# Reads of the turned softmax blocks: four reads to 96 partitions and one to 32, in place of four to 32

## The chip, the cores and the metric

The kernel runs on one core of a Trainium2 chip. The metric is the time of one execution on the device in microseconds (us). TensorE (PE) does the matrix products; VectorE (DVE), ScalarE (ACT) and GpSimd (POOL) do the elementwise work; SyncE (SP) issues every transfer, and 16 DMA engines of the core carry them out.

## The reference: what is computed

Attention with rotary positions for 8 batches x 8 heads, 576 positions, head size 64, and on its output a channel mix, all in float32:

```python
q_rot, k_rot = rotate(q), rotate(k)
scores = scale * q_rot @ k_rot.T;  attn = softmax(scores);  x = attn @ v      # per batch and head
x_prev = x shifted by one position                                            # 512 channels
xk = mu_k * x + (1 - mu_k) * x_prev;   xr = mu_r * x + (1 - mu_r) * x_prev
k = relu(xk @ w_k);  v = (k * k) @ w_v;  r = sigmoid(xr @ w_r);  out = r * v
```

## The kernel before, in words

Heads are worked in pairs, 32 pairs in all (8 batches x 4). For a pair, `plan_prep` loads and rotates keys and queries; `plan_unit` makes the scores on PE (L417) in nine tiles of 128 queries x 576 keys (five blocks of query columns, `c` = 0 to 4, two heads each, the last shared by both), takes the row maximum on DVE (L428) and the exponential on ACT (L438).

PE needs these exponentials with the keys on partitions, so they have to be turned. For the first four pairs (`EARLY`) PE turns them itself. For the other 28 pairs DVE turns them only within blocks of 32x32 (L443), into a tile `p` of 128 partitions x 18 blocks x `WG[g]` numbers, and the rest of the turning is done by a round trip through memory in `plan_move`:

- `move_out` (L504) writes `p` to a DRAM tile `turned`, 128 rows of 18 blocks. This is done in two parts a pair, `g` = 0 (block columns 0 and 1, 128 numbers a block, 1152 KB) and `g` = 1 (2, 3 and 4; 160 numbers a block, 1440 KB).
- `move_in` (L509) reads it back into a tile `rows`, where a partition holds one key position of a block. There are four reads a part, one for each strip of 32 partitions. Blocks are dealt to the strips as 5, 5, 4 and 4 (`STRIPS`).

`rows` then is the moving operand of the product with the values (PE `av`, L534; 20 matmuls a part), and its result is divided by the row sums (`rb`, loaded by DMA from a small DRAM tile `inv`). There is one `rows` tile per part and one `p` tile per part, so the reads of a part for the next pair wait until PE has consumed this pair's, and two DRAM tiles `turned` per part. The channel mix (L614 to L616, three products for each of its matrices, high and low halves) of a batch runs between the attention of the next one.

What sets the order: nothing is scheduled by the hardware. `Plan.issue` plays the program through with the costs and latencies in `Plan.LATENCY`, `act`, `dve`, `pool` and in `Plan.dma` (rate and issue cost of a transfer), and takes the ready operation with the lowest rank; ranks are made from the tables `R`, `EARLY_R`, `PB`, `MB` and the `B_` numbers. The order it finds is the order in which the instructions are written out for each engine, and each engine runs its own list strictly in that order. All transfers are in the list of SP. Besides the waits for their data, the transfers of the built program share eight semaphores in turn, so a transfer is issued only when the one eight places ahead of it has landed.

On the host, `value_blocks` lays out the values' rows in the order in which `rows` holds the key positions.

Of the kernel before, what the change touches and what calls it, by code (L numbers as in the profile page):

```python
# [22 lines left out]
P = 128  # L23
# [1 line left out]
PLAIN = 9  # L25
GROUPS = ((0, 1), (2, 3, 4))
WG = (128, 160)
STRIPS = ((0, 5), (5, 5), (10, 4), (14, 4))
EARLY = 4
R = dict(k=-170.58, q=-121.86, v=-302.6, cs=1164.53, mu=991.11, ld=1958.72, rope0=549.92, rope1=1861.93,  # L30
         rope2=137.07, split0=1585.28, split1=-369.49, u0=-285.6, u1=-146.91, u2=-135.16, u3=-245.03, u4=-224.69,
         mx=-295.32, ex=-799.79, tp=638.63, di=170.09, dm=471.79, da=86.98, dw=-1486.25, dr2=1804.88, av=1680.01,
         ah=108.11, nr=-491.67, ev=-709.36, m0=142.77, mh=-13.55, mk=-153.7, mr=282.14, ms=158.17, mx1=-19.12,
         mx2=219.25, mx3=-908.53, mg=21.82, mv=16.35, dr=-380.32, key0=-1186.84, key1=1101.65, key2=400.27,
         gate0=1557.76, gate1=-659.69, wk0=-28.46, wk1=-245.65, wr0=-326.36, wr1=175.07, wv0=-137.55, wv1=337.66)
EARLY_R = dict(k=-564.0, q=-1170.11, v=-343.8, ld=-1562.58, rope0=293.9, rope1=424.08, rope2=-27.38,
               split0=-678.82, split1=947.24, u0=48.92, u1=-764.8, u2=-518.62, u3=-170.28, u4=-518.36, mx=320.33,
               ex=-960.19, tp=-251.82, di=-478.7, dm=-397.13, da=-510.21, dw=-405.45, dr2=471.62, av=-248.39,
               ah=506.21, nr=448.89, ev=-1023.97)
PB = (-1701.39, 236.47, -547.89, 58.95, 176.83, -159.49, -34.46, 8.57)  # L40
B_COPY, B_ROPE, B_SPLIT, B_LOW, B_MIX, B_SQUARE, B_RELU = -1101.5, -35.23, 368.36, 1453.79, 1150.37, -1080.99, -375.92
MB = (-168.94, -271.8, -134.14, -339.86, 331.16, -643.19, 619.37, 428.48)
CY = 12
BUFS = dict(nat=2, kh=2, kl=1, qh=2, ql=1, vs=1, pe=4, pe3=8, p0=1, p1=1, s=2, s3=3, nm=6, sums=2, rb=1, pt0=1, pt1=1, t=2, xT=5, raw=1, we=1, wm=1, mxf=2, mxh=5, mxl=5, acc=2, hr=2, kkh=8, kkl=8, rt=3)

# [5 lines left out]
def act(n):  # L51
    return 0.833 * n + 100


def dve(n):
    return 1.04 * n + 70


def dve2(n):
    return 0.52 * n + 75  # L60
# [12 lines left out]
class Plan:  # L73
# [16 lines left out]
    def op(self, engine, rank, cost, fn, after=(), uses=()):  # L90


        o = len(self.ops)
        if isinstance(engine, str):
            engine, fn = {engine: (cost, 0, engine == "G")}, lambda e, fn=fn: fn()
        opens = [s for s in uses if s.opener is None]
        for s in uses:
            s.users += 1
        for s in opens:
            s.opener = o  # L100
        self.ops.append((engine, rank, None, fn, tuple(after), tuple(uses), opens))
        return o

    def dma(self, rank, nbytes, fn, after=(), uses=(), rate=360):

        o = self.op("S", rank, 610, fn, after, uses)
        return self.op("D", rank, nbytes / rate, lambda: None, [o], uses)

    def issue(self):
# [92 lines left out]
def rope_attention_channel_mix(ctx, tc, qt, kt, v, cs, mu, w_k, w_v, w_r, out):  # L202
# [3 lines left out]
    nc = tc.nc  # L206
    B, NP, _, _, S = kt.shape
# [32 lines left out]
    def one(n, bias=0.0):  # L240

        return {"A": (act(n) + 30, 0, False), "V": (dve2(n), bias, True)}
# [8 lines left out]
    op, dma, Slot = plan.op, plan.dma, plan.slot  # L251
# [24 lines left out]
    rows_t = [const.tile([P, 4, 5, n], F32, name=f"rows_{n}") for n in WG]  # L276
# [98 lines left out]
    def plan_prep(t, b, g):  # L375
        d = live[b, g]
        d["r"] = EARLY_R if PAIRS.index((b, g)) < EARLY else R
        d["bg"], d["plain"] = (b, g), PAIRS.index((b, g)) < PLAIN
        first = PAIRS[0] == (b, g)
        plan_rope(t + d["r"]["k"], d, "k", kt[b, g], tables["cs"], d["plain"], -339.0 if first else t + d["r"]["k"] + d["r"]["ld"])  # L380
        plan_rope(t + d["r"]["q"], d, "q", qt[b, g], tables["cs"], d["plain"], -289.0 if first else t + d["r"]["q"] + d["r"]["ld"])
        sv = d["sv"] = Slot("vs")

        def load_v():
            d["vf"] = values_t[sv.index % BUFS["vs"]]
            nc.sync.dma_start(d["vf"], v[b, g])

        d["v"] = dma(t + d["r"]["v"] + d["r"]["ld"], P * 4 * 10 * D, load_v, [], [sv])
# [83 lines left out]
    def plan_move(t, d):  # L472


        ss, sr = d["ss"], Slot("rb")
        w = {}

        def inverse():
            V.tensor_scalar_add(d["sums"][:, 0:9], d["sums"][:, 0:9], 1e-9)
            V.reciprocal(d["sums"][:, 0:9], d["sums"][:, 0:9])  # L480
            V.tensor_copy(d["sums"][:, 9:10], d["sums"][:, 4:5])
            V.transpose(d["sums"], d["sums"])

        def write():
            w["dram"] = dram.tile([4, 32, 32], F32, tag="inv", name="inv", bufs=4)
            nc.sync.dma_start(w["dram"].rearrange("a u n -> (a u) n"), d["sums"])

        def read(x):
            if "rb" not in d:
                d["rb"] = sb.tile([P, 4, 160], F32, tag="rb", name="rb", bufs=BUFS["rb"])  # L490
            src = w["dram"][:, 5 * x:5 * x + 5, :].rearrange("a u n -> a (u n)").unsqueeze(0).to_broadcast([D, 4, 160])
            nc.sync.dma_start(d["rb"][(up, dn)[x]], src)

        o = op("V", t + d["r"]["nr"], 500, inverse, [d["E", u] for u in range(9)], [ss])
        o = dma(t + d["r"]["dw"], P * 128, write, [o], [ss])
        d["R"] = [dma(t + d["r"]["dr2"] + 0.1 * x, D * 4 * 640, lambda x=x: read(x), [o], [sr]) for x in range(2)]
        d["sr"] = sr

        if d["early"]:
            return  # L500

        def move_out(g):
            w["p", g] = dram.tile([P, 18, WG[g]], F32, tag=f"turned{g}", name="turned", bufs=2)
            nc.sync.dma_start(w["p", g].rearrange("p b n -> p (b n)"), d["p", g].rearrange("p b n -> p (b n)"))  # L504

        def move_in(g, s):
            at, n = STRIPS[s]
            src = w["p", g].rearrange("(a i) b n -> i a (b n)", a=4)[:, :, at * WG[g]:(at + n) * WG[g]]
            nc.sync.dma_start(rows_t[g][32 * s:32 * s + 32, :, 0:n, :].rearrange("p a j n -> p a (j n)"), src)  # L509

        for g, cs in enumerate(GROUPS):
            ready = [d["T", u] for c in cs for u in ((4,) if c == 4 else (c, c + 5))]
            o = dma(t + d["r"]["dm"] + d["r"]["da"] * g, P * 18 * 4 * WG[g], lambda g=g: move_out(g), ready, [d["sp", g]])
            for s in range(4):
                d["M", g].append(dma(t + d["r"]["dm"] + d["r"]["da"] * g + d["r"]["di"], P * STRIPS[s][1] * 4 * WG[g], lambda g=g, s=s: move_in(g, s), [o], [d["spt", g]]))

    N0 = S // 2

    def plan_values(t, d):
# [4 lines left out]
        for g in range(2):  # L524
# [18 lines left out]
            def divided_last(x):  # L543
                r = (up, dn)[x]
                acc = w[1][:, 0:384].rearrange("p (a n) -> p a n", a=4)[r, :, 80 - 80 * x:96 - 80 * x]
                V.tensor_tensor(out=d["x"][r, 513:S + 1].rearrange("p (a n) -> p a n", n=16), in0=acc, in1=d["rb"][r, :, 128 + 16 * x:144 + 16 * x], op=ALU.mult)

            o = op("T", t + d["r"]["av"] + d["r"]["ah"] * g, 2350 + 540 * g, products, d["M", g] + [d["v"]], [s_a, d["sv"], d["spt", g]])
            e[g] = [op("V", t + d["r"]["ev"] + d["r"]["ah"] * g, dve(256) + 30, divided, [o] + d["R"], [s_a, sx, d["sr"]])]
            if g:  # L550
                e[g] += [op("V", t + d["r"]["ev"] + d["r"]["ah"] * g + 0.1 * x, dve(64) + 30, lambda x=x: divided_last(x), [o] + d["R"], [s_a, sx, d["sr"]]) for x in range(2)]
        z = op("G", t + d["r"]["ev"], 110, lambda: G.memset(d["x"][:, 0:1], 0.0), [], [sx])
        d["X", 0], d["X", 1] = e[0] + e[1] + [z], e[0] + e[1]

    def plan_attention():
        for pi, bg in enumerate(PAIRS):
            plan.group = 2 * pi
            d, t = live[bg], PT * pi + (PB[pi] if pi < len(PB) else 0)
            plan_prep(t, *bg)
# [4 lines left out]
            for c in range(5):  # L564
                plan.group = 2 * pi + 0.1 * c
                plan_unit(t + (EARLY_R if pi < EARLY else R)[f"u{c}"], d, c)
            plan.group = 2 * pi
# [7 lines left out]
    def plan_mix(t, b, half, which, f, hold):  # L575
# [24 lines left out]
        o = op({"A": (act(n) + 130, 0, False), "V": (dve2(n) + 60, B_MIX, True)}, t, 0, previous, d["X", half] + [rest], [sx, s_f])  # L600
        o = op({"V": (dve(n) + 60, 0, True)}, t + R["mx1"], 0, mixed, [o], [sx, s_f])
        h = op(one(n, B_SPLIT), t + R["mx2"], 0, high, [o], [s_f, s_h])
# [102 lines left out]
    for b in range(B):  # L705
        plan_channel_mix(b, 4 * PT * b + R["m0"] + MB[b], 4 * PT * (b + 1) + R["m0"] + MB[b])
    with tc.manual_schedule():
# [65 lines left out]
```

## Time and profile before

| | |
|---|---|
| median of 3 runs | 1089.62 us (1087.89 to 1099.95) |
| the profiled execution's own time | 1090.39 us |
| its span, first to last instruction | 1088.6 us |
| PE busy | 958.2 us (88%) |
| DVE / ACT / POOL busy | 75% / 51% / 46% |
| DMA traffic | 231.72 MB, 213 GB/s over the span, 75.2% of the 16 engines' time |
| mean granted TensorE clock | 0.953 of full speed |

The span is what the profile's times are counted in; the profiled execution's own time is 1.8 us more. DMA's share is the mean over the 16 engines: it says how long packets were under way, not how fast they went, so it is read beside the GB/s of the same stretch.

### The profile page before, as it was taken

How to read it: one execution, taken by the hardware profiler on the slowest of the kernel's cores; microseconds unless marked ns; L12 is line 12 of the kernel's file. 1: busy time of each engine (PE TensorE's matmuls, PEld its weight loads, DVE VectorE, ACT ScalarE, POOL GpSimd, SP SyncE). 2: the span in 40 equal slices, each digit the busy share in tenths (PEclk: the TensorE clock that was granted, in tenths of full speed). 3: DMA queues.
4: the chain of work that ended last, by engine and by line, in shares of the span. 5: the costliest groups of instructions: out<-in, count | busy, mean ns of one | idle time of the engine just before them, and what ended most of it. 6: DMA issues, size and time to landing. Idle time of an engine off the chain costs nothing.

```text
span 1088.6 us, 18700 instructions
## 1 busy us (share of the span) xinstructions
PE 958.2 (88%) x6866; PEld 778.6 (72%) x6866; DVE 816.1 (75%) x1419; ACT 551.0 (51%) x1356; POOL 498.9 (46%) x502
## 2 busy tenths in 40 slices
PE   2788778658979999989999999999999999988898
PEld 1454456437758888868888888777777978777888
DVE  6998997798866798767988899869786966434542
ACT  2566645445454566545656665547545653414133
POOL 4644356643464474545645465529353742201111
PEclk9999879757999999999999999999999999999999
DMA  5434499964899769998998799998999597790000
GB/s 183 156 126 158 131 300 292 289 225 162 216 265 257 194 221 248 236 276 259 292 307 237 241 225 273 262 288 268 266 279 272 187 240 214 179 221 11 11 23 22
DMA packets 92731, 231.72 MB, mean 213 GB/s; under 512 B 13152, under 2 KB 37728, under 8 KB 85472
## 3 DMA queue, kind: packets, MB, share of 16 engines
q1 hardware_dynamic: 92640, 230.53, 75.2%
q8 instruction: 54, 0.88, 0.4%
q14 instruction: 37, 0.30, 0.1%
HBM read 146.21 MB, written 84.28 MB: 212 GB/s over the span
## 4 chain that ended last, share of the span: by engine, by line
PE 60%; DMA 20%; DVE 13%; ACT 3%; issue 3%; POOL 1%; SPq 1%; DVEq 0%; ACTq 0%; POOLq 0%
PE scores L614 14%; PE av L534 12%; PE scores L616 11%; PE scores L615 11%; PE scores L417 9%; DMA rows<-turned 8%; DVE nm L428 2%; DVE p L443 2%; DMA rb<-inv 2%; DMA values<-in_v 2%; DMA out_dram<-rt 2%; DMA xk<-in_kt 2%; DMA turned<-p 2%; PE turn L463 1%; DMA xq<-in_qt 1%
## 5 line engine op out<-in xcount | busy, mean ns | idle before, releaser
L438 ACT ACTIVATE pe<-scores,nm 128x576 f32<-128x576 f32 x252 | 184.6, 737 | 121.3 <-DVE nm L428 117.2
L428 DVE TENSOR_REDUCE nm<-scores 128x1 f32<-128x576 f32 x288 | 205.5, 747 | 38.8 <-PE scores L417 37.8
L443 DVE STREAM_TRANSPOSE p<-pe 128x576 f32<-128x576 f32 x252 | 186.3, 760 | 10.5 <-ACT pe L438 10.1
L534 PE MATMUL av<-rows,values 128*64 128x320 f32 (+1 forms) x1280 | 175.3, 423 | 20.4 <-issue 5.2
L417 PE MATMUL scores<-kh,qh 64*128 64x288 f32 x738 | 145.3, 428 | 48.8 <-ACT pe L438 29.6
L614 PE MATMUL scores<-mxh,wk_h 128*128 128x288 f32 x496 | 156.8, 316 | 14.7 <-ACT hr L631 7.6
L614 PE MATMUL scores<-kkh,wv_h 128*128 128x288 f32 x480 | 148.0, 308 | 14.3 <-ACT rt L661 8.2
L254 POOL TENSOR_TENSOR mxl<-mxf,mxh 128x288 fp32r<-128x288 f32 x90 | 78.7, 876 | 173.0 <-ACT mxh L258 143.3
L534 PEld LDWEIGHTS av<-rows,values 128*64 128x64 f32 x1280 | 91.8, 141 | 83.9 <-issue 31.0
L417 PEld LDWEIGHTS scores<-kh,qh 64*128 64x128 f32 x738 | 81.7, 207 | 98.0 <-ACT pe L438 41.9
L615 PE MATMUL scores<-mxl,wk_h 128*128 128x288 f32 x496 | 146.9, 296 | 1.1 <-POOL mxl L254 1.1
L616 PE MATMUL scores<-mxh,wk_l 128*128 128x288 f32 x496 | 146.6, 296 | 0.0
L616 PE MATMUL scores<-kkh,wv_l 128*128 128x288 f32 x480 | 143.4, 299 | 1.5 <-POOL wv_l L254 1.5
L615 PE MATMUL scores<-kkl,wv_h 128*128 128x288 f32 x480 | 143.1, 298 | 0.0
L254 POOL TENSOR_TENSOR kkl<-hr,kkh 128x288 fp32r<-128x288 f32 x101 | 90.0, 902 | 90.2 <-ACT kkh L258 67.8
L614 PEld LDWEIGHTS scores<-mxh,wk_h 128*128 128x128 f32 x496 | 93.8, 189 | 37.1 <-ACT hr L631 13.1
L254 POOL TENSOR_TENSOR xk<-xk,turns 128x576 f32<-128x576 f32 x46 | 70.9, 1553 | 91.4 <-DMA xk<-in_kt 73.7
L614 PEld LDWEIGHTS scores<-kkh,wv_h 128*128 128x128 f32 x480 | 91.6, 191 | 27.4 <-ACT rt L661 13.7
L254 POOL TENSOR_TENSOR xq<-xq,turns 128x128 f32<-128x128 f32 (+1 forms) x96 | 98.9, 1048 | 17.5 <-DMA xq<-in_qt 17.5
L590 DVE SCALAR_TENSOR_TENSOR mxf<-xT,mu_t,mxf 128x288 f32<-128x288 f32 x128 | 90.1, 718 | 10.7 <-ACT mxf L585 10.0
L615 PEld LDWEIGHTS scores<-mxl,wk_h 128*128 128x128 f32 x496 | 94.0, 189 | 1.5 <-POOL mxl L254 1.3
L616 PEld LDWEIGHTS scores<-mxh,wk_l 128*128 128x128 f32 x496 | 93.8, 189 | 0.2 <-POOL wk_l L254 0.2
(110 smaller groups left out, 1860.9 us busy)
## 6 DMA issues: line engine op xcount, KB each, us to landing
turned<-p SPq DMA_DIRECT2D x28, 1440.0 KB, 8.1
rows<-turned SPq DMA_DIRECT2D x112, 320.0 KB, 9.8
turned<-p SPq DMA_DIRECT2D x28, 1152.0 KB, 6.8
rows<-turned SPq DMA_DIRECT2D x56, 400.0 KB, 8.8
xq<-in_qt SPq DMA_DIRECT2D x32, 640.0 KB, 6.6
xk<-in_kt SPq DMA_DIRECT2D x32, 576.0 KB, 5.2
rows<-turned SPq DMA_DIRECT2D x56, 256.0 KB, 9.0
values<-in_v SPq DMA_DIRECT2D x32, 320.0 KB, 6.3
```

What stands on the lines that cost most here:

```text
L254: (V if e == "V" else G).tensor_tensor(out=out, in0=a, in1=b, op=op)
L417: T.matmul(w[x][:, h, 0:H], lhsT=kind(d[q][r, c * P:(c + 1) * P]), rhs=kind(d[k][r, h * H:(h + 1) * H]), start=i == 0, stop=i == len(todo) ...
L428: V.tensor_reduce(out=w["nm", x], in_=w[x][:, :, 0:H], op=ALU.max, axis=AX.XY, negate=True)
L438: A.activation(w["p", x].rearrange("p (h n) -> p h n", h=2), w[x][:, :, 0:H], AF.Exp, bias=w["nm", x], scale=1.0, accum_out=d["sums"][:, u ...
L443: V.transpose(d["p", g][:, :, at:at + 32], w["p", x].rearrange("p (b n) -> p b n", n=32))
L463: T.transpose(a[i][0:n, k * P:(k + 1) * P], w["p", x][:, j * P:j * P + n], early["ident"])
L534: T.matmul(acc[(up, dn)[x], :, to:to + n], lhsT=d["vf"][:, 5 * x + j, :], rhs=rows_t[g][:, :, j, n * x:n * x + n], start=j == 0, stop=j == 4)
L590: V.scalar_tensor_tensor(out=x["f"], in0=d["x"][:, half * n + 1:half * n + n + 1], scalar=mu_t[:, m:m + 1], in1=x["f"], op0=ALU.mult, op1= ...
L614: T.matmul(w["a"], lhsT=w_h[:, i, sl], rhs=x["h"], start=(i == 0), stop=False)
L615: T.matmul(w["a"], lhsT=w_h[:, i, sl], rhs=x["l"], start=False, stop=False)
L616: T.matmul(w["a"], lhsT=w_l[:, i, sl], rhs=x["h"], start=False, stop=(i == count - 1))
```

## The change

`move_in` reads a part with five transfers in place of four. Blocks are dealt to the strips as 5, 5, 5 and 3. For each of the four groups of 32 rows of `turned` (`a` = 0 to 3) one wide read takes blocks 0 to 14 to partitions 0 to 95; a fifth, narrow read takes blocks 15 to 17 of all rows to partitions 96 to 127. The host lays out the values to suit. `Plan.dma` now counts 400 bytes a nanosecond and 500 ns an issue (360 and 610 before), and all numbers of the rank tables are new, so the written order of every engine is new. The products, the elementwise work and the bytes moved are the same; some elementwise operations change engine. `STRIPS` was the constant `((0, 5), (5, 5), (10, 4), (14, 4))`.

```diff
-    def dma(self, rank, nbytes, fn, after=(), uses=(), rate=360):
+    def dma(self, rank, nbytes, fn, after=(), uses=(), rate=400):
-        o = self.op("S", rank, 610, fn, after, uses)
+        o = self.op("S", rank, 500, fn, after, uses)
...
-R = dict(k=-170.58, q=-121.86, v=-302.6, cs=1164.53, ...
+R = dict(k=-46.24, q=-112.99, v=167.3, cs=1791.75, ...
...
-        def move_in(g, s):
-            at, n = STRIPS[s]
-            src = w["p", g].rearrange("(a i) b n -> i a (b n)", a=4)[:, :, at * WG[g]:(at + n) * WG[g]]
-            nc.sync.dma_start(rows_t[g][32 * s:32 * s + 32, :, 0:n, :].rearrange("p a j n -> p a (j n)"), src)
+        def move_in(g, a):
+            rows = w["p", g].rearrange("(a i) b n -> i a b n", a=4)
+            if a < 4:
+                src = rows[:, a, 0:15].rearrange("i (s j) n -> s i (j n)", s=3)
+                nc.sync.dma_start(rows_t[g][0:96, a].rearrange("p j n -> p (j n)"), src)
+            else:
+                nc.sync.dma_start(rows_t[g][96:128, :, 0:3].rearrange("p a j n -> p a (j n)"), rows[:, :, 15:18].rearrange("i a j n -> i a (j n)"))
...
-            for s in range(4):
+            for a in range(5):
...
-        rows = np.full((4, 5, 32), S)
-        for s, (at, n) in enumerate(STRIPS):
-            rows[s, :n] = 32 * at + np.arange(32 * n).reshape(n, 32)
+        rows = np.minimum(32 * np.arange(20).reshape(4, 5, 1) + np.arange(32), S)
```

The new order shows best in SP's list, which holds every transfer. In its rows `turned<-p` is `move_out`, `rows_85<-turned` is a read of part 0 and `rows_86<-turned` one of part 1; the figures are the destination's partitions and numbers. The first place is the first pairs that move through memory. Before, SP's list read:

```order
L492 DMA rb<-inv 64x4x160 x2
L504 DMA turned<-p 128x2880
L504 DMA turned<-p 128x2304
L291 DMA raw<-in_w_v 128x1024
L509 DMA rows_86<-turned 32x4x800 x2
L509 DMA rows_86<-turned 32x4x640 x2
L509 DMA rows_85<-turned 32x4x640 x2
L509 DMA rows_85<-turned 32x4x512 x2
```

At the same place it now reads:

```order
L491 DMA rb<-inv 64x4x160 x2
L290 DMA raw<-in_w_r 128x1024
L503 DMA turned<-p 128x2880
L503 DMA turned<-p 128x2304
L509 DMA rows_86<-turned 96x1x800 x4
L511 DMA rows_86<-turned 32x4x480
L290 DMA raw<-in_w_v 128x1024
L509 DMA rows_85<-turned 96x1x640 x4
L511 DMA rows_85<-turned 32x4x384
```

Both writes still stand ahead of the reads of either part; each part has five reads where it had four, and one load of weights moved from between writes and reads to between the two parts' reads.

The second place lies in the middle of the program. Before, with one pair's part 1 and the next pair's part 0:

```order
L504 DMA turned<-p 128x2880
L386 DMA values_84<-in_v 128x640
L509 DMA rows_86<-turned 32x4x800 x2
L509 DMA rows_86<-turned 32x4x640 x2
L492 DMA rb<-inv 64x4x160 x2
L504 DMA turned<-p 128x2304
L509 DMA rows_85<-turned 32x4x640 x2
L509 DMA rows_85<-turned 32x4x512 x2
```

Now, at about the same pair:

```order
L503 DMA turned<-p 128x2880
L509 DMA rows_85<-turned 96x1x640 x4
L511 DMA rows_85<-turned 32x4x384
L385 DMA values_84<-in_v 128x640
L491 DMA rb<-inv 64x4x160 x2
L509 DMA rows_86<-turned 96x1x800 x4
L511 DMA rows_86<-turned 32x4x480
L673 DMA out_dram<-rt 128x288
L503 DMA turned<-p 128x2304
```

The write of part 1 now stands ahead of part 0's five reads, and the write of the next pair's part 0 stands behind part 1's five reads, where it stood behind four.

More of the change, by code (lines that the diff above doesn't have):

```diff
@@ L27 @@
 WG = (128, 160)
-STRIPS = ((0, 5), (5, 5), (10, 4), (14, 4))
 EARLY = 4
[L30 to L41, printed above, removed]
@@ L42 @@
-MB = (-168.94, -271.8, -134.14, -339.86, 331.16, -643.19, 619.37, 428.48)
+R = dict(k=-46.24, q=-112.99, v=167.3, cs=1791.75, mu=1264.72, ld=1640.88, rope0=668.83, rope1=2170.31,
+         rope2=211.53, split0=2202.72, split1=-693.2, u0=-108.39, u1=-45.48, u2=97.67, u3=-159.77, u4=-101.54,
+         mx=-380.59, ex=-996.03, tp=699.01, di=289.95, dm=353.77, da=300.36, dw=-1881.33, dr2=1719.07, av=2521.55,
+         ah=37.68, nr=-329.79, ev=-753.5, m0=163.4, mh=-16.68, mk=-24.16, mr=458.27, ms=166.92, mx1=123.09,
+         mx2=293.74, mx3=-969.99, mg=19.94, mv=13.82, dr=-638.28, key0=-1508.07, key1=1346.18, key2=6.54,
+         gate0=1608.26, gate1=-632.21, wk0=-90.95, wk1=-286.28, wr0=-674.72, wr1=347.38, wv0=-150.67, wv1=699.56)
@@ new lines @@
+EARLY_R = dict(k=-310.88, q=-1355.07, v=-331.38, ld=-1622.22, rope0=79.01, rope1=567.18, rope2=2.18,
+               split0=-1418.42, split1=1048.63, u0=262.56, u1=-1137.39, u2=-761.37, u3=-324.26, u4=-789.59,
+               mx=563.5, ex=-1246.54, tp=-462.09, di=-476.12, dm=-336.66, da=-381.54, dw=-472.89, dr2=453.49,
+               av=-108.63, ah=991.69, nr=711.42, ev=-1376.42)
+PB = (-2105.41, -72.54, -662.78, -122.25, 227.08, -309.22, -249.69, -51.84)
+B_COPY, B_ROPE, B_SPLIT, B_LOW, B_MIX, B_SQUARE, B_RELU = -971.16, -56.64, 275.68, 1563.02, 1219.56, -1021.28, -501.08
@@ L43 @@
+MB = (-91.7, -221.08, 59.62, -939.17, 511.62, -723.89, 612.38, 501.23)
 CY = 12
@@ L513, in plan_move @@
             o = dma(t + d["r"]["dm"] + d["r"]["da"] * g, P * 18 * 4 * WG[g], lambda g=g: move_out(g), ready, [d["sp", g]])
-            for s in range(4):
-                d["M", g].append(dma(t + d["r"]["dm"] + d["r"]["da"] * g + d["r"]["di"], P * STRIPS[s][1] * 4 * WG[g], lambda g=g, s=s: move_in(g, s), [o], [d["spt", g]]))
+            for a in range(5):
+                d["M", g].append(dma(t + d["r"]["dm"] + d["r"]["da"] * g + d["r"]["di"], (96 * 5 if a < 4 else 32 * 24) * 4 * WG[g], lambda g=g, a=a: move_in(g, a), [o], [d["spt", g]]))
     N0 = S // 2
```

## The prediction

> **What bounds the kernel now.** First the page: busy shares, the forty slices' DMA rows, the queue, and the shares of the chain that ended last.
>
> ```profile
> span 1088.6 us, 18700 instructions
> PE 958.2 (88%) x6866; PEld 778.6 (72%) x6866; DVE 816.1 (75%) x1419; ACT 551.0 (51%) x1356; POOL 498.9 (46%) x502
> DMA  5434499964899769998998799998999597790000
> q1 hardware_dynamic: 92640, 230.53, 75.2%
> PE 60%; DMA 20%; DVE 13%; ACT 3%; issue 3%; POOL 1%; SPq 1%; DVEq 0%; ACTq 0%; POOLq 0%
> ```
>
> PE is busy for 88% and carries 60% of the chain, so TensorE sets most of the time; but DMA is second, and in the middle of the program its engines are nearly as full. So next come the transfers by group (count, KB each, us from issue to landing), and what waits for the reads that the change rewrites.
>
> ```profile
> turned<-p SPq DMA_DIRECT2D x28, 1440.0 KB, 8.1
> rows<-turned SPq DMA_DIRECT2D x112, 320.0 KB, 9.8
> turned<-p SPq DMA_DIRECT2D x28, 1152.0 KB, 6.8
> rows<-turned SPq DMA_DIRECT2D x56, 400.0 KB, 8.8
> rows<-turned SPq DMA_DIRECT2D x56, 256.0 KB, 9.0
> ...
> L509 SPq DMA_DIRECT2D rows<-turned x224: 302/430/1662, 132.4 to 968.7; - x112
> ...
>   PE av L534: 9.7, 6
> ```
>
> A read of 320 KB takes longer to land than a write of 1152 KB; yet PE waited for reads only 9.7 us in all (last row: us, times). The reads are slow but mostly hidden: there is little to win on them, and much to lose if they become the bound. How fast the DMA engines go shows in stretches where one kind of transfer rules (after the length: busy us and counts of PE, PEld, DVE, ACT and POOL, granted clock, DMA share, GB/s):
>
> ```profile
> 144.00:149.00 5.00, 2.67 (x16) 1.44 (x14) 4.97 (x9) 2.22 (x5) 3.65 (x5) 1.00 1.05 388
> 154.00:161.00 7.00, 5.95 (x33) 5.05 (x33) 6.90 (x15) 3.72 (x9) 1.57 (x2) 0.83 1.06 222
> 126.00:990.00 864.00, 785.43 (x5749) 645.27 (x5748) 667.85 (x1150) 454.18 (x1125) 421.87 (x423) 0.95 0.88 245
> 200.00:250.00 50.00, 30.28 (x108) 20.34 (x108) 45.57 (x72) 23.60 (x54) 26.63 (x23) 0.58 0.68 234
> ...
> 126.14 0.33 SPq L504 DMA_DIRECT2D turned<-p  x1
> 143.48 2.68 SPq L504 DMA_DIRECT2D turned<-p  x2
> 150.18 4.77 SPq L509 DMA_DIRECT2D rows<-turned  x8
> ```
>
> From 144 to 149 us two writes of 128 partitions run, from 154 to 161 mostly strip reads. In both the 16 engines are full (1.05, 1.06), but the first moves 388 GB/s and the second 222: **24.3 GB/s an engine against 13.9**. The third row is the stretch in which pairs move through memory: 864 us, 245 GB/s, 211.7 MB.
>
> The Trainium skill ("SBUF — State Buffer", Door 1: The DMA port swizzle) states that partitions 0 to 31 reach 8 of 16 ports, and that p and p + 32 share one; the 222 beside 388 agrees, and by it 96 partitions would serve this change, if all engines take part.
>
> **The change, part by part.** What is removed: 224 strip reads, 2 x (320 + 256 + 400 + 320) = 2592 KB a pair. What comes: 28 x 2 x 4 wide reads of 240 and 300 KB (2160 KB a pair) and 56 narrow ones of 192 and 240 KB (432 KB). Bytes are equal.
>
> The question is how many engines a wide read uses. Its source list, as built, is 3 strips, 32 rows, 640 (or 800) numbers; its destination list is 96 partitions and the same numbers. Every transfer of before has counts of 32, 64, 128 or 256 outermost on both sides, so a cut into 16 equal pieces along them always works, and the full share on 16 engines is what that looks like. Here it doesn't: sixteen pieces would be six partitions each, and six doesn't go into a strip of 32, so such a piece is no rectangle of the source list. The one cut along the outermost counts that fits both is by **three**: one strip of 32 partitions per engine, 13 engines idle. Nothing in the trace shows an outermost count that 16 doesn't divide; I take three as likeliest from the shape of the two lists, and keep sixteen as a rival.
>
> The Trainium skill ("DMA: Bandwidth & Descriptors", Why a DMA increments its semaphore by 16 and not by 1) says that the number of engines is the largest up to 16 that divides the slowest dimension larger than one of both patterns, and that these are the lowest-numbered ones: by it three, and the same three each time. No run so far shows it; the sum by it is the one that follows.
>
> On each of three engines a pair then costs:
> 1. Wide reads: 2160 x 1024 / 3 = 737,280 bytes. At 24.3 GB/s 30.4 us, at 13.9 GB/s 53.1 us. Which rate is open. For the fast one speaks that three engines are few; for the slow one that each writes 32 neighbouring partitions, as the strip reads do. Neither row is nearer, so I take the middle, **41.8 us**.
> 2. Everything else: 211.7 MB less 74.3 MB of old reads plus 12.4 MB of narrow ones is 149.8 MB; by 16 engines and 28 pairs 334 KB, at 24.3 GB/s **13.8 us**.
> 3. A gap: reads wait for their own write to land, and where that write stands behind the other part's reads (once a pair in the new order, the second place above) the three engines empty between. The nearest rows are a lone output write and the issue of a read (430 ns, above):
>
> ```profile
> out_dram<-rt SPq DMA_DIRECT2D x13, 144.0 KB, 1.8
> ```
>
> Landing 1.8, issue 0.4, first data at most 1.8: **4 us** a pair, between 2 and 8 (both parts).
>
> Together 59.6 us a pair against (968.7 - 132.4) / 27.5 = 30.4 us now; 28 pairs are 1669 us. The lead-in up to the first move (126 us) stays, as does the end: from the last read's landing, some 9 us after 968.7, to 1088.6 is 111 us. 126 + 1669 + 111 = 1906 us of span; the profiled execution took 1.8 us beyond its span (1090.39), and the runs' median is 0.8 us under it: **about 1910 us** (lead-in, end and those 1.8 us together are 239 us, 240 below).
>
> What lies beside it costs nothing while the three engines bound: the 56 additional issues, 56 x 0.43 = 24 us on SP, which waits for landings anyway; the new order on PE, DVE, ACT and POOL, whose busy time (PE 785 us in that stretch) fits twice into 1669. PE's clock may fall: at 30.28 busy us of 50 it was granted 0.58. Then 785 x 0.95 / 0.58 is 1286 us, still under. If the cover were gone, as with sixteen engines, order and issues would be worth some 1% either way. SP's list is in order and a transfer also waits for the one eight before it; that wait exists now:
>
> ```profile
> SPq L509 <- DMA rows<-turned: 20.4, 23, 1.5
> ```
>
> With reads that queue for tens of us it will hold back loads and output writes as well, and their readers (POOL and DVE for keys and queries) will wait; that is inside the bound, not on top.
>
> **The rivals.**
> - *Sixteen engines, faster reads* (the other side: faster). If the cut is finer, 61.9 MB go at 388 in place of 222 GB/s: 279 us of DMA time become 160. PE's waits for reads (9.7 us) are the least that shrinks: 0.43 x 9.7 = 4 us. At most the chain's share for reads, 8%, 87 us, shrinks as much: 37 us.
>
> ```profile
> PE scores L614 14%; PE av L534 12%; PE scores L616 11%; PE scores L615 11%; PE scores L417 9%; DMA rows<-turned 8%; DVE nm L428 2%; DVE p L443 2%; DMA rb<-inv 2%; DMA values<-in_v 2%; DMA out_dram<-rt 2%; DMA xk<-in_kt 2%; DMA turned<-p 2%;
> ```
>
>   That gives 1053 to 1086, midway 1070 us. It decides from about eight engines up: 3 x 30.4 / 8 + 13.8 + 4 is 29 us, under the 30.4 us that a pair takes now, and PE bounds again. For it speak the slow strip rows; against it the shape of the lists.
> - *Sixteen engines, and five issues eat it*: 24 us of issue, none hidden, 1114 us at worst, some 1095 likelier. Against it: SP is idle most of the time.
> - *Three engines, each at full rate*: 28 x (30.4 + 13.8 + 4) + 240 = 1590 us. *All at the strip rate*: 28 x (53.1 + 13.8 + 4) + 240 = 2225 us. Both are inside the forecast.
>
> By what the Trainium skill's page "SBUF — State Buffer" says of p and p + 32, in the section named above, the first two of the three engines would share ports and take the slow row's rate: 2225 us. No run so far shows two engines alone on one port.
>
> **How the numbers follow.** Three engines 0.87, of which 0.37 near the middle rate and 0.25 near either end; sixteen and faster 0.10; sixteen and no gain or slower 0.03. This kernel's runs tell no change from one of about 1%. Faster by over 1%: 0.07, within: 0.05, slower: 0.88. The ends of the three-engine case: fast rate, gap 2 us, 28 x 46.2 + 240 = 1534; but slices of before, from 125 to 150 us, run at about 428 GB/s (26.8 an engine, so 27.5 and 12.5 us), which gives 1416:
>
> ```profile
> GB/s 0 151 301 408 405 428 398 295 248 292 270 74 8 98 225 299 205 194 188 241 237 205 173 328 388 426 412 413 385 365 285 334 303 431 442 424 442 387 446 398
> ```
>
> Slow rate, gap 8 us: 28 x 74.9 + 240 = 2337. From 1415 to 2340 holds about 0.82; the rest is mostly the sixteen-engine case, which stays outside.
>
> **What would show it.** Right: the whole run's GB/s falls to about 232 / 1.9 = 122, and DMA's slices to threes or fours, since 3 of 16 are full and 13 are a quarter busy; wide reads land 20 to 40 us after issue; PE `av` waits for `rows` for hundreds of us; PE's busy share falls to half, its clock with it. Step 1 is wrong in size if the pair takes 48 or 71 us, not 60; step 3 if DMA slices show pauses of over 8 us a pair. Wrong altogether: wide reads landing in 5 to 8 us with slices still at 7 to 9, which is sixteen engines.

## The result: half as much again

The changed kernel takes 1636.02 us (median of 4 runs, 1632.83 to 1639.49) against 1092.96 us for the kernel before on the same chip: a ratio of 1.496, 95% interval 1.486 to 1.506. The forecast was 1910 us, from 1415 to 2340: slower, by the mechanism that it gave, and 274 us less slow than it said.

The page of the changed kernel, the lines that answer to those of before:

```profile
span 1633.2 us, 18811 instructions
PE 1050.7 (64%) x6866; PEld 840.0 (51%) x6866; DVE 825.6 (51%) x1427; ACT 553.8 (34%) x1353; POOL 491.0 (30%) x497
DMA  5444455435543444543454434544444444342000
DMA packets 90715, 231.71 MB, mean 142 GB/s; under 512 B 11136, under 2 KB 42880, under 8 KB 83456
q1 hardware_dynamic: 90624, 230.52, 42.0%
DMA 38%; PE 18%; SPq 17%; DVE 5%; issue 3%; ACT 1%; POOL 1%; DVEq 0%; ACTq 0%; POOLq 0%
```

No engine looks full any more: PE fell from 88% to 64%, and DMA, which now leads the chain, from 75.2% to 42.0% of its time. That is the trap of this profile. The DMA share is a mean over 16 engines, and a mean of 42% can be three engines that are hardly ever free and thirteen that mostly are. Two stretches show it bare (length, busy us and counts of PE, PEld, DVE, ACT and POOL, granted clock, DMA share, GB/s):

```profile
190.00:195.00 5.00, 0.00 (x0) 0.00 (x0) 0.00 (x0) 0.00 (x0) 0.00 (x0) 0.50 0.19 77
1032.00:1039.00 7.00, 0.00 (x0) 0.00 (x0) 1.32 (x3) 0.13 (x1) 1.44 (x2) 0.69 0.19 76
```

In both PE does nothing, while DMA is at 0.19 of 16 engines, which is 3, and moves 76 to 77 GB/s, **some 25.3 GB/s an engine**. In the first stretch every data packet is one of 3200 bytes, so the three engines carry wide reads of part 1 and nothing else. In the second they mostly work off older transfers: of the 122 data packets that start in it, 18 are of a write of `p` (11520 bytes), 24 of a load of queries (5120), 48 of a load of keys (2304), 20 of a load of values (2560), and only the last 12 of the next wide reads (3200). SP had issued four wide reads just before and stood in them, as its timeline shows. The instructions of the wide reads (min, median, max ns, first and last start) took 2.6 times the 430 ns of the strip reads before, those of the narrow reads still longer:

```profile
1027.53 12.80 SPq L509 DMA_DIRECT2D rows<-turned  x4
...
L509 SPq DMA_DIRECT2D rows<-turned x224: 686/1116/7793, 133.3 to 1499.0; - x112
L511 SPq DMA_DIRECT2D rows<-turned x56: 331/3215/7427, 136.6 to 1503.3; - x56
```

The packets count it as well. The trace of before has 8,928 packets of 4 bytes for its 558 transfers, 16 for each. The changed kernel has 614 transfers and 6,912 such packets: 390 x 16 for all others leaves 672 for the 224 wide reads, **three each**. And of the 1373 us from 132 to 1505, at least three packets of SP's queue were under way for 1272, exactly three for 639.

Who waits is spread out (us in total, times, longest):

```profile
POOL xq L253 <- DMA xq<-in_qt: 299.6, 21, 27.5
...
ACT pe L437 <- DVE nm L427: 284.3, 77, 18.3
DVE xq L253 <- DMA xq<-in_qt: 179.1, 16, 18.9
PE av L536 <- DMA rows<-turned: 166.3, 16, 16.7
DVE xT L543 <- DMA rb<-inv: 138.1, 10, 21.9
```

The readers of queries (POOL and DVE) and of row sums wait as long as the product does, though these loads use all sixteen engines. The stretch from 1032 us shows one way to it. SP had issued the load of queries at 1020.77, and 104 of its 128 packets had started by 1028; the last 24, three of its sixteen shares, stood in line on the three engines and ended at 1037.0. POOL then went on, after 16.1 us of waiting:

```profile
1037.56 3.53 POOL L253 TENSOR_TENSOR xq<-xq,turns 128x512 f32<-128x512 f32 x3 [16.11 <-DMA xq<-in_qt]
```

How much of all the waiting comes from this, and how much from SP issuing a load late, isn't told apart.

### The profile page after: what moved, and what is told of

Same layout as the page of the kernel before. It is cut to its first block, busy times and chain, and to the rows that moved or that the text cites. A ratio compares the mean times of both kernels' runs of the same rounds, so it can differ in the third digit from the quotient of the medians.

```text
span 1633.2 us, 18811 instructions
## 1 busy us (share of the span) xinstructions
PE 1050.7 (64%) x6866; PEld 840.0 (51%) x6866; DVE 825.6 (51%) x1427; ACT 553.8 (34%) x1353; POOL 491.0 (30%) x497
## 2 busy tenths in 40 slices
DMA packets 90715, 231.71 MB, mean 142 GB/s; under 512 B 11136, under 2 KB 42880, under 8 KB 83456
## 4 chain that ended last, share of the span: by engine, by line
DMA 38%; PE 18%; SPq 17%; DVE 5%; issue 3%; ACT 1%; POOL 1%; DVEq 0%; ACTq 0%; POOLq 0%
DMA rows<-turned 17%; SPq L509 10%; DMA xq<-in_qt 8%; DMA turned<-p 5%; PE scores L616 5%; PE scores L617 4%; PE scores L618 4%; SPq L511 4%; PE av L536 3%; DMA out_dram<-rt 3%; DMA rb<-inv 2%; DMA xk<-in_kt 2%; PE scores L416 1%; SPq L491 1%; DVE p L442 1%
## 5 line engine op out<-in xcount | busy, mean ns | idle before, releaser
L536 PE MATMUL av<-rows,values 128*64 128x320 f32 (+1 forms) x1280 | 223.0, 509 | 246.1 <-DMA rows<-turned 166.3
L536 PEld LDWEIGHTS av<-rows,values 128*64 128x64 f32 x1280 | 114.2, 171 | 333.3 <-issue 296.7
L616 PE MATMUL scores<-kkh,wv_h 128*128 128x288 f32 x480 | 158.2, 330 | 104.6 <-DVE rt L672 67.8
L253 POOL TENSOR_TENSOR xq<-xq,turns 128x512 f32<-128x512 f32 (+1 forms) x90 | 95.1, 1072 | 299.6 <-DMA xq<-in_qt 299.6
L616 PEld LDWEIGHTS scores<-kkh,wv_h 128*128 128x128 f32 x480 | 100.6, 210 | 119.0 <-DVE rt L672 71.0
L617 PE MATMUL scores<-kkl,wv_h 128*128 128x288 f32 x480 | 152.1, 317 | 7.3 <-POOL kkl L253 7.3
L253 DVE TENSOR_TENSOR xq<-xq,turns 128x128 f32<-128x128 f32 (+1 forms) x38 | 34.6, 926 | 179.2 <-DMA xq<-in_qt 179.1
L616 PE MATMUL scores<-mxh,wr_h 128*128 128x288 f32 x248 | 84.0, 339 | 38.9 <-DVE rt L672 13.3
L543 DVE TENSOR_TENSOR xT<-av,rb 128x256 f32<-128x256 f32 x64 | 25.9, 416 | 157.5 <-DMA rb<-inv 138.1
L617 PEld LDWEIGHTS scores<-kkl,wv_h 128*128 128x128 f32 x480 | 101.0, 210 | 7.6 <-POOL kkl L253 7.5
```

The source lines that it names most:

```text
L253: (V if e == "V" else G).tensor_tensor(out=out, in0=a, in1=b, op=op)
L536: T.matmul(acc[(up, dn)[x], :, to:to + n], lhsT=d["vf"][:, 5 * x + j, :], rhs=rows_t[g][:, :, j, n * x:n * x + n], start=j == 0, stop=j == 4)
L543: V.tensor_tensor(out=xo, in0=acc, in1=d["rb"][:, :, 64 * g:64 * g + 64].rearrange("p a (c n) -> p a c n", n=32), op=ALU.mult)
L616: T.matmul(w["a"], lhsT=w_h[:, i, sl], rhs=x["h"], start=(i == 0), stop=False)
L617: T.matmul(w["a"], lhsT=w_h[:, i, sl], rhs=x["l"], start=False, stop=False)
```

## The experiments

### The same transfers with the rows in front

Only the walk of a wide read's source is turned round, with the host's values permuted to suit; the written order of every engine is that of the changed kernel.

```diff
-                src = rows[:, a, 0:15].rearrange("i (s j) n -> s i (j n)", s=3)
+                src = rows[:, a, 0:15].rearrange("i (s j) n -> i s (j n)", s=3)
...
-        strips = rows.transpose(1, 0, 2).reshape(5 * P)
+        strips = np.concatenate([rows[:3].transpose(1, 2, 0).reshape(5, 96), rows[3]], axis=1).reshape(5 * P)
```

> The changed kernel with one thing turned round: a wide read's source is walked rows first (32 rows, 3 strips, 640 numbers) instead of strips first, and the host permutes the values to suit. Order of every engine, count of transfers and bytes are those of the changed kernel. Theory (the count of 3 in front confines a wide read to 3 engines): 32 in front can be cut in 16, so the time falls back to that of before or below, 1050 to 1100 us, the DMA share of 42% no longer has slices of 75 GB/s, and packets under 512 B come back up by 13 per wide read, 2912 in all. Rival (five reads a part, the new written order or the window of eight costs the time): stays at 1500 us or more.

Measured: 1078.16 us (1074.8 to 1081.58), 0.985 of before (0.979 to 0.991): far under the changed kernel, and a little faster than before. Its page, its reads and their issue:

```profile
span 1079.7 us, 18811 instructions
DMA packets 93627, 231.72 MB, mean 215 GB/s; under 512 B 14048, under 2 KB 45792, under 8 KB 86368
q1 hardware_dynamic: 93536, 230.53, 69.5%
rows<-turned SPq DMA_DIRECT2D x140, 240.0 KB, 6.8
rows<-turned SPq DMA_DIRECT2D x112, 300.0 KB, 7.2
L509 SPq DMA_DIRECT2D rows<-turned x224: 541/590/1706, 137.7 to 959.6; - x112
```

Packets under 512 B rose from 11136 to 14048, by 2912, which is 224 x 13. Bytes, transfers and order are equal, so the 558 us between the two kernels come from the walk of the wide reads alone: with it go the number of engines and which partitions an engine writes. That the number of engines is what counts is shown by the packets here and by the kernels with fewer bytes below. The reads now land in 7 us where the old strip reads took 9 to 10 (the row of 240 KB counts 28 narrow reads too, the one of 300 KB wide reads alone), DMA's share is 69.5% for 75.2%, and the issue of a wide read takes 590 ns, not 1116.

### The tables of before with both kinds of wide read

All rank tables and `Plan.dma`'s numbers are put back, once with strips in front as in the changed kernel, once with rows in front:

```diff
-    def dma(self, rank, nbytes, fn, after=(), uses=(), rate=400):
+    def dma(self, rank, nbytes, fn, after=(), uses=(), rate=360):
-        o = self.op("S", rank, 500, fn, after, uses)
+        o = self.op("S", rank, 610, fn, after, uses)
...
-R = dict(k=-46.24, q=-112.99, v=167.3, cs=1791.75, ...
+R = dict(k=-170.58, q=-121.86, v=-302.6, cs=1164.53, ...
```

> The changed kernel's reads (strips first) with the rank tables and the planner's rate and issue cost of before. Theory of 3 engines: the order hardly matters, since 28 x (29.5 us of wide reads + 13 us of the rest) bound the stretch: 1560 to 1720 us. Rival (the new order does the harm): near 1100 us.

> Rows-first wide reads with the rank tables and planner numbers of before. Theory: all 16 engines, so 1060 to 1100 us; against the run with the new tables it says what the new order is worth once the reads don't bound: within 2% either way. Rival (new order is the harm): clearly faster than the rows-first kernel with the new tables, by over 200 us.

Measured: 1613.34 us (one run) with strips in front, 1080.7 us (1077.5 to 1082.59; 0.987 of before, 0.980 to 0.993) with rows in front. Where the reads don't bound, the new order is worth nothing that can be told apart: 1078 beside 1081. Where three engines bound, the kernel with the new order took 1636 and the one run with the old order 1613, 1.4% less; with one run the size of that is loose, but it is far from the 543 us that were lost. The rival that the order did the harm is out.

### Fewer bytes on the three engines

Each wide read takes 3 blocks of 5, then 1 of 5; in the second kernel of one block the rows are in front.

```diff
-                src = rows[:, a, 0:15].rearrange("i (s j) n -> s i (j n)", s=3)
-                nc.sync.dma_start(rows_t[g][0:96, a].rearrange("p j n -> p (j n)"), src)
+                src = rows[:, a, 0:15].rearrange("i (s j) n -> s i (j n)", s=3)[:, :, 0:3 * WG[g]]
+                nc.sync.dma_start(rows_t[g][0:96, a, 0:3].rearrange("p j n -> p (j n)"), src)
```

> The changed kernel with strips first, but each wide read takes 3 of its 5 blocks (the other key positions aren't refreshed, so part of the attention is left out); order and number of transfers stay. Theory: the three engines' bytes set the pace, so 40% of 29.5 us a pair goes, 28 x 11.8 = 330 us: about 1300 us (1250 to 1350). Rival (a fixed cost per wide read, as of issue or landing, sets it): stays within 80 us of 1636.

> The changed kernel, strips first on three engines, with wide reads of 1 block in place of 5 (most of the other key positions aren't refreshed, part of the attention is left out); order and number of transfers stay. From the whole kernel and the three-block one the pace is 20 us a pair plus 25 GB/s: 5.9 + 20 = 26 us, under the 30.4 us that PE takes. Theory: the bound goes back to PE, 1050 to 1110 us, not the 976 us that a straight line through the two times would give. Rival (the pace per pair has no floor near 30 us): below 1020 us.

> The rows-first kernel (16 engines) with wide reads of 1 block in place of 5, the rest left out as above. It asks how much reads still cost once all engines take part. Theory (they are hidden): within 1% of the rows-first kernel's 1078 us, 1065 to 1085. Rival (DMA still takes a share of the time): 1040 us or less.

Measured: 1306.15 and 1053.07 us (one run each) and 1058.8 us (1053.51 to 1059.61, 0.967 of before, 0.959 to 0.974). The pages' spans and the starts of the wide reads, first with three blocks, then with one:

```profile
span 1304.3 us, 18811 instructions
L509 SPq DMA_DIRECT2D rows<-turned x224: 685/752/6140, 138.9 to 1177.2; - x112
```

```profile
span 1051.1 us, 18837 instructions
PE 947.0 (90%) x6866; PEld 766.0 (73%) x6866; DVE 827.8 (79%) x1427; ACT 553.1 (53%) x1353; POOL 488.1 (46%) x497
L509 SPq DMA_DIRECT2D rows<-turned x224: 685/717/2957, 131.5 to 931.3; - x112
```

A pair takes (1499.0 - 133.3) / 27.5 = 49.7 us in the changed kernel, 37.8 with three blocks, 29.1 with one. From five blocks to three 294,912 bytes an engine go and 11.9 us: 24.8 GB/s, close to the 25.3 of the quiet stretches. From three to one the same bytes go but only 8.7 us: there PE (90%) is the bound again, with three engines still in use, and the time is that of sixteen engines with the same bytes (1053 beside 1059). So in this kernel three engines do harm through the bytes that they carry, and not through a fixed cost of each read.

The third of these missed its theory and its rival. With 16 engines, four fifths less in the wide reads saved 19 us (1.8%), where under 1% or over 38 us had been expected: in the rows-first kernel the reads still cost a little.

### Reads that don't wait for their own write

Each part reads what the pair before wrote, which a third DRAM tile keeps.

```diff
-            w["p", g] = dram.tile([P, 18, WG[g]], F32, tag=f"turned{g}", name="turned", bufs=2)
+            w["p", g] = dram.tile([P, 18, WG[g]], F32, tag=f"turned{g}", name="turned", bufs=3)
+            written[g].append(w["p", g])
+            w["from", g] = written[g][-2:][0]
...
-            rows = w["p", g].rearrange("(a i) b n -> i a b n", a=4)
+            rows = w["from", g].rearrange("(a i) b n -> i a b n", a=4)
```

> The changed kernel, strips first, whole wide reads, but each part reads what the pair before wrote (a third DRAM tile keeps it), so no read waits for its own write to land; it computes with another pair's exponentials. It asks what the gap of some 7 us a pair is, that the forecast took as 4. Theory (it is the wait for the write, with the three engines empty): up to 28 x 7 = 196 us less, 1440 to 1560 us. Rival (it is the wait for PE to free the rows tile, or SP held up in issuing): 1600 us or more.

Measured: 1627.5 us (one run), 8.5 us less, as the rival had it. What SP waited for such writes before a wide read, first in the changed kernel, then here (us in total, times, longest):

```profile
SPq L509 <- DMA turned<-p: 56.0, 9, 15.7
...
SPq L513 <- DMA turned<-p: 6.9, 3, 2.6
```

49 us of that wait are gone, and the time fell by some half a percent. The theory falls: SP's wait for a part's own write is mostly not what holds the three engines up.

The 7 us in question were also too much, as the next section shows.

## Why the prediction was right, and where its sizes were off

**Three engines.** Right, and shown twice: by 672 packets for 224 reads, and by the kernel with the rows in front. The argument from the shape (a piece must fit both lists; 96 / 16 = 6 doesn't go into 32) gave the right number.

By the rule of the Trainium skill's page "DMA: Bandwidth & Descriptors" (Why a DMA increments its semaphore by 16 and not by 1) three was the count, as largest number up to 16 that divides 3 and 96. The trace agrees: three small packets a wide read and a DMA share of 0.19. With the rows in front it is 16, which divides 32 and 96, and the 2912 additional packets agree too. The argument and the page's rule give the same counts for both lists, so no run here tells them apart.

**Step 1, the wide reads: the failed size.** The prediction took the middle between a fast and a slow row, 41.8 us a pair, a rate that no row showed. The runs show the fast end: 737,280 bytes at 25.3 GB/s are 29.1 us. The slow row (13.9 GB/s an engine) belongs to sixteen engines that write the same 32 partitions at once; three engines with 32 partitions each don't meet it. This one term is 28 x 12.7 = 356 us too much, more than the whole error of 274; step 2 took some of it back. That the range held the result all the same is due to its width: it ran from the fast row to the slow one.

The Trainium skill's page "SBUF — State Buffer" (Door 1: The DMA port swizzle) puts p and p + 32 on one port, so the first two engines share their ports. The prediction concluded from it that they would take the slow rate, which the page doesn't state. The 25.3 GB/s of each engine doesn't agree with that conclusion, and the rows of before spoke against it: 32 partitions took 222 GB/s from sixteen engines, and two engines bring 51 GB/s. Whether two engines slow each other when they write the same port at the same moment was not tried.

**Step 2, everything else: too small.** The share 42.0% of 1633.2 us is 686 us for a mean engine. Wide reads make 3/16 x 28 x 29.1 = 153 of them. The lead-in and the end take 70, by these rows:

```profile
0.00:130.00 130.00, 88.22 (x516) 52.64 (x516) 113.69 (x193) 66.61 (x154) 73.03 (x68) 0.95 0.46 147
1505.00:1633.20 128.20, 105.15 (x703) 93.87 (x699) 46.34 (x104) 33.24 (x81) 15.60 (x19) 0.94 0.08 27
```

What is left is 463 us, 16.5 a pair for 13.8 forecast: not all of it runs at the rate of the writes from which the 13.8 came. Packets of 640 bytes, for one, take 32 ns at the median in the changed kernel's trace, 20 GB/s an engine.

**Step 3, the gap: right in size, wrong in cause.** 49.7 - 29.1 - 16.5 leaves 4.1 us for 4 forecast. (The 7 us in the last experiment came from taking 13 for step 2.) This split takes the wide reads at 25.3 GB/s throughout; their packets of 3200 bytes took 129 ns at the median but 144 in the mean, so some of the 16.5 and the 4.1 may belong to step 1. In the trace of the changed kernel no packet of the queue is under way for 77 of the 1373 us, 2.8 us a pair, which fits the 4.

But the cause given, reads that wait for their write, is worth 8.5 us in all. The trace shows what SP stood before in those 77 us: for 25 an output write (L673), for 15 a write of `p`, for 9 a wide read. And such pauses are not new: the trace of before has 83 us without a packet from 132 to 978 us, 3.0 a pair. What closing them would save was not tried, so the cause of the gap stays open.

**The ends and the cover.** The lead-in was as before (first read at 133 us, before at 132). From the last read's issue to the end it took 130 us, where the prediction had counted 111 from a landing some 9 us after the issue: that read still had to get through the line (`av` ends at 1526; from there to the end it is 107 us, as before). PE's clock fell to 0.79 between 130 and 1505 us, and its work rose to 857 us; both fitted under the bound, as said:

```profile
130.00:1505.00 1375.00, 857.36 (x5653) 693.52 (x5653) 665.57 (x1131) 453.94 (x1119) 402.32 (x410) 0.79 0.45 152
```

**The signs named ahead.** GB/s fell to 142 (122 forecast, in a time that came out shorter), the slices to fours and fives. A pair took 49.7 us, near the 48 that was named as the sign of step 1 being wrong in size. PE's busy share fell to 64% and not to half, since the time came out shorter than forecast; its clock fell with it, to 0.81 over the run. PE's wait for `rows` was 166 us, but most waiting stood at the loads of queries, 479 us on POOL and DVE: the prediction mentioned them and didn't expect them to lead. Landing times of wide reads aren't listed for the changed kernel.

**The rival on the other side** was priced at 1053 to 1086 us, and the kernel that realises its condition, sixteen engines, took 1078. Its point of decision ("from about eight engines up") was about engines for full reads; one block on three engines confirms the same limit by bytes, since 26 us on an engine is under PE's 29 to 30.

## What to carry to other kernels

Before widening a transfer, look at the outermost count of both access lists as they are built, not at the partitions of the tile: one walk of the same bytes (3 x 32) took 1636 us, the other (32 x 3) 1078. If no engine seems full but DMA leads the chain, take a quiet stretch and multiply its DMA share by 16: 0.19 is three engines, and 76 GB/s over three is an engine at full speed. And a planner that counts bytes at one rate, as `Plan.dma` does, can't see this; here the order that it found was worth under 2% in either setting.

## What the runs showed that was not expected

SP's issue of a transfer isn't a fixed cost: with three engines full, a wide read's issue took 1116 ns at the median and up to 7793, the narrow read's 3215, against 590 and 586 when the rows stood in front and all engines took part. Most of this goes with how full the three engines are: with strips in front and one block in place of five, the medians were 717 and 630.

```profile
L511 SPq DMA_DIRECT2D rows<-turned x56: 319/586/1339, 140.3 to 960.2; - x56
```

And a read of 300 KB to 96 partitions, all engines taking part, lands in 7.2 us, while 320 KB to 32 partitions took 9.8 us. With the order of before, the five reads a part with the rows in front are worth 1.3% of this kernel (0.7 to 2.0); with the new order it is 1.5% (0.9 to 2.1).
